# Reordering products, sums and MLP work at the seams of a fused attention and GELU-MLP kernel

## The chip, the cores and the metric

The kernel runs on one core of one Trainium2 chip. The metric is device time in microseconds (us) for one execution, as the median of several runs. The engines have these short names in the profile: PE is TensorE (matrix products; PEld its weight loads), DVE is VectorE, ACT is ScalarE, POOL is GpSimd, SP is SyncE, which here issues DMA transfers.

## The reference: what is computed

Threshold attention over 8 batches, 8 heads, 576 tokens and 64 columns a head, then a two-layer MLP with exact GELU on the 4608 resulting rows of 512. All of it is float32. Cut to what matters:

```python
scores = scale * q @ k.T                                  # per batch and head, 576 x 576
scores = where(scores >= max(scores) - tau, scores, -1e9)
attn   = exp(scores - max(scores)); attn /= (sum(attn) + 1e-9)
x      = (attn @ v) laid out as 4608 x 512
h      = x @ w_in                                         # 512 -> 2048, "layer one"
g      = 0.5 * h * (1 + erf(h / sqrt(2)))
out    = g @ w_out                                        # 2048 -> 512, "layer two"
```

## The kernel before

The kernel has two parts. In the first, attention runs pair of heads by pair of heads (32 pairs of 5 slots each: 160 slots). For each pair the exponentials are transposed through DMA into tiles pT, and `weigh_v` multiplies them with v into x^T in PSUM; ACT copies it to `xall`, and POOL divides it by the row sums. In between, a pacing function (`GOAL`, `fill`) feeds PE with plain MLP products for the blocks of 256 tokens that are complete: `hT` is layer one, `o_ps` layer two. It handles 8 of the 18 blocks.

The second part, `last_blocks`, does the other 10 blocks in two groups of five, with a seven-product multiplication (Strassen's scheme in Winograd's form): fewer products on PE, paid for with sums of operands. Layer one uses it on two levels (seven outer products, each a chain of seven products with 320 columns), layer two on one level. Each group has four steps j; a step is layer one (`layer_in`), then layer two (`layer_out`) for a quarter of the hidden columns. The pieces that the change touches:

```python
    def x_sums():

        room = list(tail["x_room"])
        x = xall[:, 0:len(AWAY), :, :].rearrange("p b (k h) (o t) -> p b k h o t", k=2, o=2)
        part = {f"b{k + 1}{o + 1}": x[:, :, k, :, o, :] for k in range(2) for o in range(2)}
        right = tail["right"] = {}

        def inner(eng, name, v, keep=False):
            b = {(h, i): v[:, :, h, i * RUN:(i + 1) * RUN] for h in range(2) for i in range(2)}
            t1, t2, t4 = (room.pop(0) for _ in range(3))
            t3 = room.pop(0) if keep else b[0, 1]
            right[name] = {"b11": b[0, 0], "b21": b[1, 0], "b22": b[1, 1], "t1": t1, "t2": t2, "t3": t3, "t4": t4}
            yield eng, lambda: sub(eng, t1, b[0, 1], b[0, 0])
            yield eng, lambda: sub(eng, t3, b[1, 1], b[0, 1])
            yield eng, lambda: sub(eng, t2, b[1, 1], t1)
            yield eng, lambda: sub(eng, t4, b[1, 0], t2)

        def outer(eng, out, a, b):
            for h in range(2):
                yield eng, lambda h=h: sub(eng, out[:, :, h, :], a[:, :, h, :], b[:, :, h, :])

        t1, t2, t4 = tail["t_x"]
        yield from outer(vec, t1, part["b12"], part["b11"])
        yield from inner(vec, "b11", part["b11"])
        yield from inner(vec, "t1", t1, True)
        yield from outer(vec, t2, part["b22"], t1)
        yield from inner(vec, "t2", t2, True)
        yield from outer(vec, part["b12"], part["b22"], part["b12"])
        yield from inner(vec, "t3", part["b12"])
        yield from inner(vec, "b22", part["b22"])
        yield from outer(vec, t4, part["b21"], t2)
        yield from inner(pool, "b21", part["b21"])
        yield from inner(pool, "t4", t4)
# ...
def taken(to, x, first):
        if first is None:
            nc.scalar.copy(to, x)
        else:
            add(vec, to, first, x)

waiting = []      # the two products of a chain that are issued inside the next one
beside = []       # sums that are issued one by one between products

    def step(which):

        if which is not None:
            which()
        if beside:
            beside.pop(0)[1]()
        while beside and beside[0][0] is pool:
            beside.pop(0)[1]()

    def chain(n, m, takes, done=None, runs=1):

        x, y = bank("sc", n), bank("mm", n)
        v = bank("mm", n) if "m2" in m else None

        def one_of(name, to, start):
            def run():
                product(to.rearrange("p (b t) -> p b t", b=runs) if runs > 1 else to, m[name], start)
                for t in takes[name]:
                    taken(t[0], to, t[1])
                if done:
                    done(name)
            return run

        before = waiting.pop(0) if waiting else (None, None)
        step(one_of("m1", x, True))
        step(before[0])
        step(one_of("m7", y, True))
        if v is not None:
            step(one_of("m2", v, True))
        step(before[1])
        step(one_of("m6", x, False))
        step(one_of("m4", y, False))
        waiting.append((one_of("m5", x, False), one_of("m3", x, False)))
# ... layer_in: seven outer chains; the last one is outer("s4", "b22", U, U, gelus_of(U))
    def g_sums():

        c, g = tail["c"], tail["g"]
        for t in range(2):
            g11, g21, g12, g22 = (c[:, i, :, t, :] for i in range(4))
            gs1, gs2 = g[:, 0, :, t, :], g[:, 1, :, t, :]
            yield vec, lambda gs1=gs1, a=g21, b=g22: add(vec, gs1, a, b)
            yield vec, lambda g21=g21, a=g11: sub(vec, g21, a, g21)
            yield vec, lambda gs2=gs2, a=gs1, b=g11: sub(vec, gs2, a, b)
            eng = (vec, pool)[t]
            yield eng, lambda eng=eng, g12=g12, b=gs2: sub(eng, g12, g12, b)

    def spread(items):
        for eng, run in items:
            yield eng, run
            if eng is vec:
                yield vec, lambda: None
# ... layer_out, with MT = 5 row tiles and HD = 256 columns:
        before = waiting.pop(0)
        for m in range(MT):
            v = bank("mm", HD)

            def run(m=m, v=v):
                product(v, rows(g12, m, w(1, 0)), True)
                taken(lo[m][:, 0:HD], v, None if first else lo[m][:, 0:HD])

            if m == 0:
                sums = list(g_sums())
                sums.pop(0)[1]()
            step(run)
            if m < 2:
                step(before[m])
            if m == 1:
                beside.extend(sums[:2])
                beside.extend(spread(sums[2:]))
        between(-1)
        for m in range(MT):
            l0, l1, h0, h1 = lo[m][:, 0:HD], lo[m][:, HD:2 * HD], hi[m][:, 0:HD], hi[m][:, HD:2 * HD]
            new = (lambda d: (d, None if first else d))
            takes = {"m1": [(l0, l0)], "m7": [new(h1)], "m6": [new(h0)], "m4": [(h0, h0)], "m5": [(h1, h1)], "m3": [new(l1)]}
            ms = {"m1": rows(g11, m, w(0, 0)), "m7": rows(g21, m, t[:, 2]), "m6": rows(gs2, m, t[:, 1]),
                  "m4": rows(g22, m, t[:, 3]), "m5": rows(gs1, m, t[:, 0]), "m3": rows(g12, m, w(1, 1))}

            def done(name, m=m):
                if final and name == "m5":
                    store(1, m)
                if final and name == "m3":
                    store(0, m)

            chain(HD, ms, takes, done)
            between(m)
# ... last_blocks:
        x_tiles()
        sums = list(x_sums())
        for _, run in sums[:10]:
            run()
        w_out_sums(vec, 0)
        for _, run in sums[10:]:
            run()
# ...
                if m == 0 and after[1] != j:
                    beside.append((pool, lambda j=after[1]: w_in_sums(pool, j)))
                if m == 0 and after[0] != n:
                    beside.extend(x_sums())

            layer_in(j, in_layer_in)
            layer_out(GROUPS[n], j, in_layer_out, at % NJ == 0, at % NJ == NJ - 1)
# ... the pacing of plain MLP work in the attention part (BATCH * B = 160 slots, WEIGH = 2, PLAIN = 8):
    GOAL = [(-1, 0.0), (START - 1, 0.0), (BATCH - 1, 0.42)]
    GOAL += [(BATCH * (m + 2) + DIVIDE, x) for m, x in enumerate([1.92, 2.89, 3.86, 4.82, 5.79, 6.75])]
    GOAL += [(BATCH * B + WEIGH, PLAIN - 0.28)]
```

How to read it. A *product* on PE writes a PSUM bank, and `taken` moves or adds the bank to SBUF: an ACT copy where the target is new, a DVE addition otherwise. A chain has two banks x and y that accumulate: m1, then m6, m5, m3 go into x, m7 and m4 into y, and m2, which layer two's chains lack, has a bank of its own. So each product must wait until the take before it has read the bank. m5 and m3 of a chain are not issued with it; they wait in `waiting` and are issued inside the next chain. At the seam from layer one to layer two, the next "chain" is the loop over five tiles m, whose products (g12 times a block of w_out) need nothing of the last chain. `g_sums` are eight sums of GELU results that layer two needs (four for each half t). `step` runs one product and then takes one sum from `beside`.

Of the kernel before, what the change touches and what calls it, by code (L numbers as in the profile page):

```python
# [18 lines left out]
def kernel(  # L19
# [31 lines left out]
    B, H, S, D = q.shape  # L51
# [16 lines left out]
    PLAIN = N_BLK - 10  # L68
# [61 lines left out]
    sums = [att.tile([P, Q], FP32, name=f"sums{i}") for i in range(2)]  # L130
# [532 lines left out]
    def sub(eng, out, a, b):  # L663
        eng.tensor_tensor(out, a, b, op=ALU.subtract)  # L664
# [46 lines left out]
    def w_out_sums(eng, j):  # L711
        t = tail["t"]
        b11, b12 = w_out_q[:, 0, :, j, 0:HD], w_out_q[:, 0, :, j, HD:2 * HD]
        b21, b22 = w_out_q[:, 1, :, j, 0:HD], w_out_q[:, 1, :, j, HD:2 * HD]
        sub(eng, t[:, 0], b12, b11)
        sub(eng, t[:, 1], b22, t[:, 0])
        sub(eng, t[:, 2], b22, b12)
        sub(eng, t[:, 3], b21, t[:, 1])
# [29 lines left out]
# [17 lines that stand above are left out]
        def outer(eng, out, a, b):  # L765
            for h in range(2):
                yield eng, lambda h=h: sub(eng, out[:, :, h, :], a[:, :, h, :], b[:, :, h, :])

        t1, t2, t4 = tail["t_x"]
        yield from outer(vec, t1, part["b12"], part["b11"])  # L770
# [11 lines that stand above are left out]
    def product(to, pairs, start):  # L782
        for k, (l, r) in enumerate(pairs):
            nc.tensor.matmul(to, lhsT=l, rhs=r, start=start and k == 0, stop=k == len(pairs) - 1,  # L784
                             skip_group_check=not start)

    def bank(tag, n):
        if tag == "sc":
            return ps.tile([P, 2, 512], FP32, tag="sc", name="bank", bufs=2)[:, 0, 0:n]
        return ps.tile([P, 512], FP32, tag="mm", name="bank")[:, 0:n]  # L790
# [8 lines that stand above are left out]
    waiting = []  # L799
    beside = []  # L800
# [9 lines that stand above are left out]
# [87 lines left out]
# [6 lines that stand above are left out]
    def layer_out(blocks, j, between, first, final):  # L903

        c, g, t, o = tail["c"], tail["g"], tail["t"], tail["o"]
        g11, g21, g12, g22 = (c[:, i].rearrange("p f t n -> p f (t n)") for i in range(4))
        gs1, gs2 = (g[:, i].rearrange("p f t n -> p f (t n)") for i in range(2))
        lo, hi = o[:MT], o[MT:]

        def rows(z, m, w):  # L910
            return [(z[:, f, m * P:(m + 1) * P], w[:, f]) for f in range(2)]

        def w(k, d):
            return w_out_q[:, k, :, j, d * HD:(d + 1) * HD]

        def store(half, m):
            for r in range(2):
                q, b = divmod(2 * m + r, len(AWAY))
                row = blocks[b] * TOK + (2 * half + q) * RUN
                nc.sync.dma_start(out[row:row + RUN, :], o[half * MT + m][r * RUN:(r + 1) * RUN, :])  # L920
# [10 lines that stand above are left out]
                sums = list(g_sums())  # L931
                sums.pop(0)[1]()
            step(run)
            if m < 2:
                step(before[m])
            if m == 1:
                beside.extend(sums[:2])
                beside.extend(spread(sums[2:]))
        between(-1)
        for m in range(MT):  # L940
            l0, l1, h0, h1 = lo[m][:, 0:HD], lo[m][:, HD:2 * HD], hi[m][:, 0:HD], hi[m][:, HD:2 * HD]
# [14 lines that stand above are left out]
    def last_blocks():  # L956

        assert set(x_free) == {XSLOTS - 2, XSLOTS - 1}
        GROUPS[0].sort(key=x_at.get)
        x_tiles()  # L960
        sums = list(x_sums())
        for _, run in sums[:10]:
            run()
        w_out_sums(vec, 0)
        for _, run in sums[10:]:
            run()
        steps = [(n, j if n % 2 == 0 else NJ - 1 - j) for n in range(len(GROUPS)) for j in range(NJ)]
        for at, (n, j) in enumerate(steps):
            before = steps[at - 1] if at else None
            after = steps[at + 1] if at + 1 < len(steps) else None  # L970

            def in_layer_in():
                if before and before[1] != j:
                    w_out_sums(pool, j)

            def in_layer_out(m):
                if after is None:
                    return
                if m == -1 and after[0] != n:
                    for k in range(2):  # L980
                        for b, x in enumerate(GROUPS[after[0]]):
                            nc.sync.dma_start(xall[:, b, 2 * k:2 * k + 2, :], away[x][:, 2 * k:2 * k + 2, :])
# [7 lines that stand above are left out]
        while waiting:  # L990
            for f in waiting.pop(0):
                f()
        assert not beside
# [25 lines left out]
    BATCH = HP * SLOTS  # L1019
    WIDE = 5 * 2 * Q  # L1020
    WEIGH = 2
# [2 lines left out]

    GOAL = [(-1, 0.0), (START - 1, 0.0), (BATCH - 1, 0.42)]
    GOAL += [(BATCH * (m + 2) + DIVIDE, x) for m, x in enumerate([1.92, 2.89, 3.86, 4.82, 5.79, 6.75])]
    GOAL += [(BATCH * B + WEIGH, PLAIN - 0.28)]

    def goal(n):
        for (lo, x), (hi, y) in zip(GOAL, GOAL[1:]):  # L1030
# [134 lines left out]
```

## Time and profile before

| what | value |
|---|---|
| median of 3 runs | 1365.79 us (1365.21 to 1366.95) |
| span of the profiled execution | 1365.8 us, 20074 instructions |
| busy: PE / DVE / POOL / ACT | 1338.9 / 1066.8 / 634.4 / 600.3 us |
| attention with plain MLP work | 0 to about 896 us |
| the two groups in seven-product form | about 896 to 1366 us |

The profile page gives first the busy time of each engine, then the span in 40 slices with the busy tenths of each engine and the clock that TensorE was granted, then DMA, then the chain of waits that ended last, then the costliest groups of instructions. For this case the timeline (each instruction, or run of equal ones, with its start and duration) is the view that matters. In it a float32 product on PE shows as two records. Records start one after another at a fixed pitch and their ends are modelled, so a run of n records has a length of (n-1) pitches and one duration.

### The profile page before, as it was taken

How to read it: one execution, taken by the hardware profiler on the slowest of the kernel's cores; microseconds unless marked ns; L12 is line 12 of the kernel's file. 1: busy time of each engine (PE TensorE's matmuls, PEld its weight loads, DVE VectorE, ACT ScalarE, POOL GpSimd, SP SyncE). 2: the span in 40 equal slices, each digit the busy share in tenths (PEclk: the TensorE clock that was granted, in tenths of full speed). 3: DMA queues.
4: the chain of work that ended last, by engine and by line, in shares of the span. 5: the costliest groups of instructions: out<-in, count | busy, mean ns of one | idle time of the engine just before them, and what ended most of it. 6: DMA issues, size and time to landing. Idle time of an engine off the chain costs nothing.

```text
span 1365.8 us, 20074 instructions
## 1 busy us (share of the span) xinstructions
PE 1338.9 (98%) x6398; PEld 904.1 (66%) x6398; DVE 1066.8 (78%) x2062; ACT 600.3 (44%) x1024; POOL 634.4 (46%) x1085
## 2 busy tenths in 40 slices
PE   8899999999999999999999999999999999999998
PEld 6677557466466566556557557468787777877777
DVE  7998777788888888878988888863857698385665
ACT  7766537438447448448538448222201113210120
POOL 5553344454555565555555541235264503635530
PEclk9999999999999999999999999999999999999999
DMA  9987376677777787787787785400000131000003
GB/s 293 327 307 216 78 165 142 140 169 181 160 183 168 164 205 163 166 213 156 164 216 158 167 188 115 104 9 1 0 1 0 39 91 26 1 1 0 1 0 78
DMA packets 212471, 169.18 MB, mean 124 GB/s; under 512 B 113872, under 2 KB 193600, under 8 KB 212368
## 3 DMA queue, kind: packets, MB, share of 16 engines
q1 hardware_dynamic: 188224, 112.53, 37.3%
q0 software_dynamic: 23712, 55.08, 13.4%
q8 instruction: 52, 0.85, 0.3%
q14 instruction: 51, 0.42, 0.1%
q10 hardware_dynamic: 432, 0.30, 0.1%
HBM read 72.73 MB, written 12.52 MB: 62 GB/s over the span
## 4 chain that ended last, share of the span: by engine, by line
PE 84%; DVE 8%; DMA 3%; SPq 2%; ACT 1%; issue 1%; POOL 0%; DVEq 0%; ACTq 0%; POOLq 0%
PE bank L784 30%; PE hT L597 16%; PE o_ps L612 15%; PE sc L403 12%; PE xT L521 10%; PE tr L345 1%; DVE o L667 1%; DMA turned_p<-in_moe_w_in_dram 1%; DVE nmx L415 1%; DVE p L434 1%; DVE c L667 1%; DMA x<-xall 1%; DVE c L664 1%; DVE power L217 1%; ACT p L418 1%
## 5 line engine op out<-in xcount | busy, mean ns | idle before, releaser
L418 ACT ACTIVATE p<-sc,nmx 128x576 f32<-128x576 f32 x288 | 201.5, 737 | 267.1 <-DVE nmx L415 266.7
L434 DVE SCALAR_TENSOR_TENSOR p<-sc,thr,p 128x576 f32<-128x576 f32 x288 | 225.2, 815 | 64.5 <-ACT p L418 61.4
L416 POOL TENSOR_SCALAR thr<-nmx,tau_eff 128x1 f32<-128x1 f32 x288 | 89.1, 309 | 375.6 <-DVE nmx L415 374.7
L415 DVE TENSOR_REDUCE nmx<-sc 128x1 f32<-128x576 f32 x288 | 205.2, 749 | 53.9 <-PE sc L403 52.8
L597 PE MATMUL hT<-xall,w_in 128*128 128x256 f32 x1024 | 241.9, 386 | 0.0
L612 PE MATMUL o_ps<-w_out,g 128*128 128x512 f32 x512 | 238.4, 606 | 0.0
L597 PEld LDWEIGHTS hT<-xall,w_in 128*128 128x128 f32 x1024 | 189.3, 190 | 51.0 <-issue 25.4
L667 DVE TENSOR_TENSOR c<-c,bank 128x320 f32<-128x320 f32 x304 | 147.3, 487 | 44.5 <-PE bank L784 30.8
L667 DVE TENSOR_TENSOR o<-o,bank 128x256 f32<-128x256 f32 x240 | 100.6, 419 | 95.0 <-PE bank L784 94.5
L612 PEld LDWEIGHTS o_ps<-w_out,g 128*128 128x128 f32 x512 | 93.8, 191 | 110.7 <-issue 108.3
L521 PE MATMUL xT<-pT,v 128*64 128x256 f32 (+1 forms) x1280 | 164.8, 410 | 2.2 <-DMA pT<-pd_tail 2.2
L403 PE MATMUL sc<-kT,qT 64*128 64x288 f32 x960 | 159.0, 430 | 3.0 <-DVE p L434 2.4
L482 DVE STREAM_TRANSPOSE turned_p<-p 128x1152 f32<-128x1152 f32 x112 | 154.4, 1378 | 3.9
L403 PEld LDWEIGHTS sc<-kT,qT 64*128 64x128 f32 x960 | 91.1, 186 | 76.3 <-issue 62.6
L521 PEld LDWEIGHTS xT<-pT,v 128*64 128x64 f32 x1280 | 89.4, 137 | 74.6 <-issue 13.3
L784 PE MATMUL bank<-w_out,c 128*128 128x256 f32 x480 | 119.8, 380 | 1.0 <-DVE o L667 0.7
L265 POOL DMA_DIRECT2D v<-in_v_dram x208 | 110.9, 536 | 4.0 <-issue 2.0
L784 PEld LDWEIGHTS bank<-w_out,c 128*128 128x128 f32 x480 | 90.3, 190 | 19.0 <-DVE o L667 2.4
L837 ACT ACTIVATE c<-c 128x320 f32<-128x320 f32 (+1 forms) x80 | 46.9, 623 | 112.1 <-DVE c L667 112.0
L667 POOL TENSOR_TENSOR c<-c,g 128x320 f32<-128x320 f32 (+1 forms) x40 | 50.5, 1271 | 79.1 <-DVE c L667 79.1
L784 PE MATMUL bank<-t_out,g 128*128 128x256 f32 x320 | 82.8, 381 | 1.6 <-DVE o L667 1.6
L795 ACT COPY c<-bank 128x320 f32<-128x320 f32 x32 | 13.6, 425 | 159.5 <-PE bank L784 159.4
(181 smaller groups left out, 1858.5 us busy)
## 6 DMA issues: line engine op xcount, KB each, us to landing
pT<-turned_p SPq DMA_DIRECT2D x448, 160.0 KB, 3.6
pT<-pd_tail SPq DMA_DIRECT2D x112, 80.0 KB, 3.1
q<-in_q_dram POOLq DMA_DIRECT2D x104, 72.0 KB, 3.2
k<-in_k_dram POOLq DMA_DIRECT2D x104, 72.0 KB, 3.3
inv<-turned SPq DMA_DIRECT2D x54, 128.0 KB, 4.0
v<-in_v_dram POOLq DMA_DIRECT2D x156, 40.0 KB, 3.2
out_dram<-o SPq DMA_DIRECT2D x40, 128.0 KB, 2.4
xall<-in_moe_w_out_dram POOLq DMA_DIRECT2D x9, 512.0 KB, 4.8
```

The costliest lines, as they stand in the source:

```text
L265: eng.dma_start(t[r:P:4, e, 0:n, :], rows[:, r * KR:r * KR + n, :])
L403: nc.tensor.matmul(sc[e][:, h, 0:HALF], lhsT=lhsT, rhs=s["kT"][rows, at:at + HALF], start=True, stop=True)
L415: nc.vector.tensor_reduce(nmx[:, e:e + 1], sc, axis=AXIS.XY, op=ALU.max, negate=True)
L416: nc.gpsimd.tensor_scalar(thr[:, e:e + 1], nmx[:, e:e + 1], -1.0, tau_eff, op0=ALU.mult, op1=ALU.subtract)
L418: nc.scalar.activation(w[:, e * S:(e + 1) * S].rearrange("p (h s) -> p h s", h=2), sc, AF.Exp, bias=nmx[:, e:e + 1], scale=1.0)
L434: nc.vector.scalar_tensor_tensor(row, sc[e][:, :, 0:HALF], thr[:, e:e + 1], row, op0=ALU.is_ge, op1=ALU.mult, accum_out=den[e])
L482: nc.vector.transpose(turned_p[:, :, i // 2, 0:NB, i % 2 * Q:(i % 2 + 1) * Q], w.rearrange("p (e b i) -> p e b i", e=2, i=Q))
L521: nc.tensor.matmul(to, lhsT=s["v"][:, e, c, :], rhs=rhs, start=(c == 0), stop=(c == KR - 1))
L597: nc.tensor.matmul(hT[:, j % 2, :], lhsT=w_in_sb[c][:, j * P:(j + 1) * P], rhs=x_blk[n][:, c, :], start=(c == 0), stop=(c == N_DM - 1))
L612: nc.tensor.matmul(o[:, 0:d_model], lhsT=g[j][:, m * P:(m + 1) * P], rhs=w_out_sb[j], start=(j == 0), stop=(j == N_DF - 1))
L667: eng.tensor_tensor(out, a, b, op=ALU.add)
L784: nc.tensor.matmul(to, lhsT=l, rhs=r, start=start and k == 0, stop=k == len(pairs) - 1, skip_group_check=not start)
```

## The change: what it does and what it is for

There are three parts.

1. **At the seam from layer one to layer two.** Of the last chain of layer one two products are left over, m5 and m3. Before, they stood behind the first and second tile of layer two; now they stand behind the first and third. The second and third sum of `g_sums` are issued by themselves behind tiles 1 and 2, and the other five go into `beside`, each vector one with an empty place after it. The aim is to give the take of m5 time before m3 needs its bank, and to keep sums from standing in front of takes.
2. **Sums of x for the second group.** In `x_sums` each sum of `outer` (the wide ones, 640 columns) is followed by an empty place, so that two wide sums are not issued in two steps in a row. The count of sums that run at once ahead of the first group goes from 10 to 12 for that reason alone: two of the 12 are empty places.
3. **Pacing.** The goal of MLP work is raised for the slots 159 to 161, so that more plain MLP work is done ahead of the x^T product of the last pair, which waits for DMA, and less behind it.

The instructions are the same in number and kind; only their order differs. On PE, the products between the last scores (`sc` from q_tail) and the x^T of the last pair are 21 `o_ps` instead of 9, and those behind it 10 instead of 21; one `hT` product more and one `o_ps` fewer stand ahead of those scores.

```diff
@@ -765,6 +765,7 @@
         def outer(eng, out, a, b):
             for h in range(2):
                 yield eng, lambda h=h: sub(eng, out[:, :, h, :], a[:, :, h, :], b[:, :, h, :])
+                yield eng, lambda: None
 
         t1, t2, t4 = tail["t_x"]
         yield from outer(vec, t1, part["b12"], part["b11"])
@@ -931,11 +932,11 @@
                 sums = list(g_sums())
                 sums.pop(0)[1]()
             step(run)
-            if m < 2:
-                step(before[m])
-            if m == 1:
-                beside.extend(sums[:2])
-                beside.extend(spread(sums[2:]))
+            if m % 2 == 0 and m < 4:
+                step(before[m // 2])
+            if m in (1, 2):
+                sums.pop(0)[1]()
+        beside.extend(spread(sums))
         between(-1)
         for m in range(MT):
             l0, l1, h0, h1 = lo[m][:, 0:HD], lo[m][:, HD:2 * HD], hi[m][:, 0:HD], hi[m][:, HD:2 * HD]
@@ -959,10 +960,10 @@
         GROUPS[0].sort(key=x_at.get)
         x_tiles()
         sums = list(x_sums())
-        for _, run in sums[:10]:
+        for _, run in sums[:12]:
             run()
         w_out_sums(vec, 0)
-        for _, run in sums[10:]:
+        for _, run in sums[12:]:
             run()
         steps = [(n, j if n % 2 == 0 else NJ - 1 - j) for n in range(len(GROUPS)) for j in range(NJ)]
         for at, (n, j) in enumerate(steps):
@@ -1024,7 +1025,7 @@
 
     GOAL = [(-1, 0.0), (START - 1, 0.0), (BATCH - 1, 0.42)]
     GOAL += [(BATCH * (m + 2) + DIVIDE, x) for m, x in enumerate([1.92, 2.89, 3.86, 4.82, 5.79, 6.75])]
-    GOAL += [(BATCH * B + WEIGH, PLAIN - 0.28)]
+    GOAL += [(BATCH * B - 1, PLAIN - 0.44), (BATCH * B + 1, PLAIN - 0.17), (BATCH * B + WEIGH, PLAIN - 0.17)]
 
     def goal(n):
         for (lo, x), (hi, y) in zip(GOAL, GOAL[1:]):
```

## The prediction, made before the result was known

> **What bounds the kernel now.** I read the page's first two parts, then the timeline of PE and of DVE at one seam of the second part, then the same around the last x^T, and the chain of waits to see whether the pattern repeats.
>
> ```profile
> PE 1338.9 (98%) x6398; PEld 904.1 (66%) x6398; DVE 1066.8 (78%) x2062; ACT 600.3 (44%) x1024; POOL 634.4 (46%) x1085
> PE   8899999999999999999999999999999999999998
> ```
>
> PE is the bound throughout: 1365.8 - 1338.9 leaves 27 us of idle time, part of it at the two ends. No PE work is removed by the change, so all it can win is holes on PE, and they are small. To size them I go by the pitch of starts. A run of 16 records with 256 columns (second fence) takes 3.62 us, the last of them 0.38, so (3.62 - 0.38) / 15 = 0.216 us each; records of 320 columns in the same way (4 in 1.24 us, the last 0.43) 0.27, and a 512-column `o_ps` record 0.43. A product of layer two is 4 records, 0.86 us; one of layer one 2 records, 0.54 us.
>
> PE at the second seam of its kind, group one, step j = 2:
>
> ```profile
> 1036.87 1.03 PE L784 MATMUL bank<-w_out,c 128*128 128x256 f32 x4
> 1037.73 0.70 PE L784 MATMUL bank<-x,s_in 128*128 128x320 f32 x2
> 1038.27 1.03 PE L784 MATMUL bank<-w_out,c 128*128 128x256 f32 x4
> 1039.75 0.81 PE L784 MATMUL bank<-xall,s_in 128*128 128x320 f32 x2 [0.46 <-DVE c L667]
> 1040.39 3.62 PE L784 MATMUL bank<-w_out,c 128*128 128x256 f32 x16
> 1043.85 1.03 PE L784 MATMUL bank<-t_out,c 128*128 128x256 f32 x4
> 1045.14 1.13 PE L784 MATMUL bank<-t_out,g 128*128 128x256 f32 x4 [0.26 <-DVE o L667]
> 1046.20 1.13 PE L784 MATMUL bank<-t_out,c 128*128 128x256 f32 x4
> ```
>
> These are tile 0, m5, tile 1, m3, then tiles 2 to 4 and m1 of the first layer-two chain, m7, m6, m4. Tile 1 should be over at 1038.27 + 0.86 = 1039.13, but m3 starts at 1039.75 and its run is 0.1 longer: 0.72 lost. m6 should start at 1043.85 + 0.86 = 1044.71, starts at 1045.14, and each of the two rows from there is stretched by 0.1, with 0.1 more between them (1045.14 + 0.96 = 1046.10 against 1046.20): another 0.72. DVE in the same place:
>
> ```profile
> 1038.14 0.83 DVE L667 TENSOR_TENSOR g<-c 128x640 f32<-128x640 f32 x1 [0.54 <-ACT c L837]
> 1038.89 0.41 DVE L667 TENSOR_TENSOR o<-o,bank 128x256 f32<-128x256 f32 x1
> 1039.22 0.48 DVE L667 TENSOR_TENSOR c<-c,bank 128x320 f32<-128x320 f32 x1
> ...
> 1043.60 0.41 DVE L667 TENSOR_TENSOR o<-o,bank 128x256 f32<-128x256 f32 x1
> 1043.93 0.82 DVE L664 TENSOR_TENSOR c<-c,g 128x640 f32<-128x640 f32 x1
> 1044.67 0.41 DVE L667 TENSOR_TENSOR o<-o,bank 128x256 f32<-128x256 f32 x1
> ```
>
> The take of m5 (1039.22) stands behind the first sum, which waits for a GELU; m3 goes into the same bank and starts when that take ends at 1039.7. The take of m1 (1044.67) stands behind the sum at 1043.93, and m6 starts when it ends. So 1.44 us are lost here. The chain of waits has the same rows at 981, 1039, 1097, 1214, 1272 and 1330 us; at the two seams with new output tiles (924 and 1157, where ACT takes the tiles) only the first wait stands, 0.40 us each. All eight: 6 x 1.44 + 2 x 0.40 = 9.4 us.
>
> The last x^T, with an undisturbed one (849.39) to compare:
>
> ```profile
> 849.39 5.07 PE L521 MATMUL xT<-pT,v 128*64 128x320 f32 x40
> ...
> 868.96 3.34 PE L521 MATMUL xT<-pT,v 128*64 128x320 f32 x22
> 874.47 3.36 PE L521 MATMUL xT<-pT,v 128*64 128x256 f32 x18 [2.18 <-DMA pT<-pd_tail]
> ```
> ```profile
> 875.00:876.00 1.00, 1.00 (x12) 0.74 (x10) 1.00 (x2) 0.00 (x0) 0.83 (x1) 0.82 0.00 0
> 876.00:877.00 1.00, 1.00 (x7) 0.67 (x4) 0.96 (x3) 0.00 (x0) 0.00 (x0) 0.50 0.00 0
> 877.00:878.00 1.00, 1.00 (x4) 0.24 (x3) 0.97 (x4) 0.13 (x1) 0.00 (x0) 0.50 0.00 0
> 878.00:880.00 2.00, 2.00 (x4) 0.98 (x5) 1.97 (x3) 0.24 (x1) 1.68 (x2) 0.73 0.00 0
> ```
>
> PE waits 2.2 us for the last transposed tile. Then the granted clock (the number before the last two) is halved: 0.18 + 0.50 + 0.50 + 2 x 0.27 = 1.7 us of full clock lost. Together 3.9 us.
>
> The fourth place is the end of group one (1107 to 1125), where wide sums of x stand between takes: four late products of layer two, by the same pitch count 0.46, 0.34, 0.38 and 0.32, and 0.16 shortly after: 1.7 us.
>
> [...] The half clock here lasts 1.7 / 0.5 = 3.4 us[...]. [...] the take of tile 0, complete at about 1037.9 (1036.87 + 1.03), starts at 1038.89 only, behind a sum that waits. [...] a wide sum takes 0.82 us alone and 1.48 at 1107.49, beside a POOL sum. [...]
>
> **Part 1, the seams.** PE from 1036.87 with the new order, if nothing waits: tile 0, m5 at 1037.73, tile 1 at 1038.27, tile 2 at 1039.13, m3 at 1039.99, tile 3 at 1040.53, tile 4 at 1041.39, m1 at 1042.25, m7 at 1043.11, m6 at 1043.97, m4 at 1044.83. A bank is ready for its take about 0.75 us after the start of a 320-column product (0.70 + 0.04) and 1.07 after a layer-two product. DVE occupies per instruction, by the distances of starts above, 0.33 us for a tile's take, 0.40 for a layer-one take, 0.74 for a sum. In the new order, from 1038.89: tile 0, m5 (1039.22), tile 1 (1039.62), second sum (1039.96), tile 2 (1040.69), m3 (1041.03), third sum (1041.43), tile 3 (1042.17), tile 4 (1042.50), m1 (1043.32, when ready), fourth sum (1043.65), m7 (1044.39). m3 needs the take of m5: over at 1039.70, before 1039.99. m6 needs the take of m1: over at 1043.73, before 1043.97. m4 needs the take of m7: over at 1044.80, just before 1044.83. The third sum, which m6 reads, is over at 1042.2. One chain on, the leftover m3 needs a take that my walk ends 0.1 us too late. I keep 0.1 us a seam for that and the narrow m4: 6 x 1.34 = 8.0, and 0.8 for the other two seams, **8.8 us**.
>
> **Part 2, spaced wide sums.** Every empty place gives DVE one step (0.86 us) with only a 0.33 take. The tight spot is m3 of each chain: m5 is two steps ahead of it, so 1.72 - 1.07 - 0.41 = 0.24 us of slack for the take of m5. In the new order no wide sum falls between m7 and the take of m5 in layer two, so I expect nearly no loss there. But 8 more places push 14 instead of 5 vector sums and places past the end of layer two into the next layer one, whose steps are 0.54 us. There two wide sums, the second beside POOL (1.44 us in the trace now), come just ahead of a take that m3 of the second chain needs, about 0.6 us too late. Estimate: 1.7 now, 0.9 after, **0.8 us**.
>
> **Part 3, MLP work ahead of the last x^T.** Its start moves by 11 `o_ps` x 0.86 + one `hT` (2 x 0.215) = 9.9 us, to 878.9. Its second half then starts at about 881.6, and its data were there at 874.4: no wait, no half clock. x^T lasts 5.0 as at 849.39 (to 854.39, the next row), the 10 `o_ps` behind it 8.6: layer one starts at 868.96 + 9.9 + 5.0 + 8.6 = 892.5 instead of 896.5: **4.0 us**, as the 3.9 above.
>
> **Sum.** 8.8 + 0.8 + 4.0 = 13.6 us, so 1352.2; I say 1352.5.
>
> **The rivals.** (a) *The wait moves.* The change takes nothing off DVE, and the walk passes m4 by 0.03 us. If takes start only a little later, the loss of the first wait goes and that of the second stays, 6 x 0.72 = 4.3 us less gain: 1356.8. For it: DVE is without a pause from 1038.1 to 1042.8 in my walk. Against it: the old order has four sums ahead of m6, the new one three. (b) *DVE becomes late at the start of the first group.* x^T comes 6 us later in time, and DVE's second wide sum waits for it: it can go on at about 885.6 instead of 882.8, and the sums end at 894.7 instead of 891.9, while layer one starts at 892.5. Its first takes are mostly ACT copies and the first DVE take is due at 894.9, so I expect nothing; if I am wrong, 1 to 2 us, 1354. (c) *The half clock stays* although the wait goes, since earlier stretches have it too (clock 0.98 and 0.97 in the first 200 us): 1.7 us, 1354. (d) *The overflow of sums into the second group costs more* than spacing wins, because POOL's sums start some 5 us later: 1 to 2 us. In each rival the bound stays PE, and none reaches the time of before.
>
> **Range and chances.** The holes named add up to 9.4 + 1.7 + 3.9 = 15.0 us, so 1350.8 is the floor; with the spread of the measurement (1.7 us over three runs) I take 1350.5. Rivals (a) alone, or two of the small ones, give 1356 to 1357: 1356.8 as the upper end. 2% is 27 us, more than all of PE's idle time, so within 2% has 0.98, and faster or slower by more 0.01 each.
>
> **What would show it.** In the timeline after: m3 and m6 at the seams without idle ahead of them; x^T of the last pair in one unbroken run of about 5 us with a clock of 1.00 around it; the first row of layer one at about 892.5; at the group change no late products in layer two, one or two small ones in the first chains behind it. I am wrong if m4 or m6 still wait for DVE at each seam, or if ACT or DVE holds the first chains of layer one.

## The result, and the profile after

The median is 1354.66 us (1353.78 to 1355.1) against 1365.53 us of the kernel before (four executions, the three of the table above among them); the ratio is 0.9918, with a 95% interval of 0.99 to 0.9935. The prediction said 1352.5 us, between 1350.5 and 1356.8. The changed kernel was timed twice more: 0.9905 (0.9889 to 0.9922) and 0.9921 (0.9902 to 0.994). So the gain is 10.9 us by the first medians and 11 to 13 by the ratios, where my sum was 13.6; between the two profiles it is 12.6 (1365.8 to 1353.2).

First the page's busy line and, from the chain of waits, the one row that covers nearly all of the second part, both of the kernel after:

```profile
PE 1334.1 (99%) x6398; PEld 905.6 (67%) x6398; DVE 1063.0 (79%) x2062; ACT 600.7 (44%) x1024; POOL 633.7 (47%) x1085
```
```profile
893.06 454.11 PE bank L785 x1900
```

In the chain of before, each seam broke the PE rows with takes, sums and a GELU. Now PE is released by nothing but itself from 893 to 1347 us. The same seam as in the prediction (group one, j = 2), timeline of PE after; columns: start, duration, engine, line, operation, tiles, shape, records:

```profile
1031.74 1.03 PE L785 MATMUL bank<-w_out,c 128*128 128x256 f32 x4
1032.61 0.70 PE L785 MATMUL bank<-x,s_in 128*128 128x320 f32 x2
1033.14 1.89 PE L785 MATMUL bank<-w_out,c 128*128 128x256 f32 x8
1034.87 0.70 PE L785 MATMUL bank<-xall,s_in 128*128 128x320 f32 x2
1035.41 2.75 PE L785 MATMUL bank<-w_out,c 128*128 128x256 f32 x12
1038.00 1.03 PE L785 MATMUL bank<-t_out,c 128*128 128x256 f32 x4
1038.86 1.03 PE L785 MATMUL bank<-t_out,g 128*128 128x256 f32 x4
1039.74 1.13 PE L785 MATMUL bank<-t_out,c 128*128 128x256 f32 x4
```

Tiles 1 and 2 run as one row of 8, m3 follows at once (1033.14 + 8 x 0.216 = 1034.87), and m6 (1038.86) comes one product after m7. Only m4 (1039.74) is 0.02 late and 0.1 longer. The last x^T, after:

```profile
879.21 5.07 PE L521 MATMUL xT<-pT,v 128*64 128x320 f32 x40
884.21 8.85 PE L612 MATMUL o_ps<-w_out,g 128*128 128x512 f32 x20
892.89 0.70 PE L785 MATMUL bank<-xall,w_in 128*128 128x320 f32 x2
```

It is one unbroken run of 5.0 us to the next start, and layer one starts at 892.89. The clock (the number before the last two) is 1.00 in this stretch, where it fell to 0.50 before:

```profile
880.00:885.00 5.00, 5.00 (x38) 2.79 (x35) 1.05 (x2) 0.86 (x3) 1.23 (x3) 1.00 0.00 0
```

Two lengths in the trace separate the parts from the spread of executions. One goes from the start of the x^T of the last pair but one to the first product of layer one, and is 47.1 us before (849.39 to 896.52) and 43.1 after (849.76 to 892.89). The other goes from the start of the first to the start of the last product record of the second part: 464.5 before, 455.5 after. The start of that x^T itself lay anywhere from 846.9 to 852.5 us in the profiles, in kernels that are the same up to there: of the differences between profiles of equal work this is the largest, and it blurs the times. The first product of layer one, before:

```profile
896.52 0.70 PE L784 MATMUL bank<-xall,w_in 128*128 128x320 f32 x2
```

### The profile page after: what moved, and what is told of

The parts are those of the page before. It is cut to its first block, busy times and chain, and to the rows that moved or that the text cites. A ratio compares the mean times of both kernels' runs of the same rounds, so it can differ in the third digit from the quotient of the medians.

```text
span 1353.2 us, 20076 instructions
## 1 busy us (share of the span) xinstructions
PE 1334.1 (99%) x6398; PEld 905.6 (67%) x6398; DVE 1063.0 (79%) x2062; ACT 600.7 (44%) x1024; POOL 633.7 (47%) x1085
## 4 chain that ended last, share of the span: by engine, by line
PE 93%; DMA 3%; DVE 2%; SPq 1%; ACT 1%; issue 0%; POOL 0%; ACTq 0%; DVEq 0%; POOLq 0%
PE bank L785 34%; PE o_ps L612 17%; PE hT L597 17%; PE sc L403 13%; PE xT L521 11%; PE tr L345 2%; DMA v<-in_v_dram 1%; DMA x<-xall 1%; DMA xall<-in_moe_w_in_dram 1%; DMA k<-in_k_dram 1%; DVE p L434 0%; DVE nmx L415 0%; ACT p L418 0%; DVE power L217 0%; SPq L284 0%
## 5 line engine op out<-in xcount | busy, mean ns | idle before, releaser
L785 PE MATMUL bank<-t_out,c 128*128 128x256 f32 x320 | 82.7, 381 | 0.0
```

## The experiments

All ratios are to the kernel before on the same chip. The last two columns are the two lengths just named, from the profile of each run; those of timed executions are not known.

| kernel | ratio (95% interval) | x^T to layer one, us | second part, us |
|---|---|---|---|
| before_again | 1.0002 (0.999 to 1.0013) | 45.0 | 464.5 |
| pacing_only | 0.9973 (0.9963 to 0.9983) | 43.1 | 464.5 |
| seam_only | 0.994 (0.9922 to 0.9957) | 45.6 | 456.1 |
| spacing_only | 0.9987 (0.9977 to 0.9998) | 45.2 | 463.3 |
| products_only | 0.9967 (0.9956 to 0.9978) | 44.9 | 459.3 |
| sums_only | 0.9968 (0.996 to 0.9976) | 44.9 | 461.3 |
| wait_long | 1.0029 (1.0018 to 1.004) | 47.8 | 464.6 |
| after_again / after_third | 0.9905 / 0.9921 | 43.1 | 455.6 |
| tuned / tuned2 / tuned3 | 0.9909 (0.9894 to 0.9924) / 0.9934 (0.9915 to 0.9952) / 0.9902 (0.9884 to 0.992) | 43.1 | 455.0 / 454.9 / 454.2 |

**The kernel before once more** (no edit).

> The kernel before, unchanged, profiled and timed once more. The saving was 12.6 us between the two profiles (1365.8 to 1353.2) but 10.9 us between the medians. Theory A (the number of half-clock windows of 3.4 us differs between executions, 1.7 us each, wherever they fall): ratio 1.000 within noise, its executions spread over 1 to 3 us, and the longer ones have the lower mean clock (0.00125 per window). Theory B (the half clock behind the 2.2 us wait for the last x^T is itself there in some executions only): this profile shows a clock of 1.00 between 875 and 880 us and a span near 1364. If instead the half clock stands there again, A alone holds.

Its profile lasts 1364.2 us, 1.6 less than the first. Timeline of PE, then two stretches (start and end, length, busy time and records of each engine, clock, DMA share, GB/s):

```profile
869.53 3.34 PE L521 MATMUL xT<-pT,v 128*64 128x320 f32 x22
874.58 2.34 PE L521 MATMUL xT<-pT,v 128*64 128x256 f32 x18 [1.72 <-issue]
```
```profile
872.00:876.00 4.00, 2.28 (x20) 1.47 (x18) 3.93 (x9) 0.49 (x2) 1.02 (x3) 1.00 0.39 70
876.00:880.00 4.00, 4.00 (x16) 1.82 (x13) 3.93 (x6) 0.37 (x1) 2.53 (x3) 1.00 0.00 0
```

The wait is there (1.7 us), the half clock is not: the 18 records take 2.34 us instead of 3.36. So theory B holds for this execution: the half clock behind the wait belongs to some executions only. Theory A agrees with the times beside it: executions of before with mean clock 0.993 took 1368.9 us on average, those with 0.996 1365.8 (8 and 9 of the 45 timed beside `wait_long`).

**Each part alone.**

```diff
# pacing_only: the GOAL line of the change, nothing else
# seam_only: the lines of layer_out of the change, nothing else
# spacing_only: the empty place in outer(), and 12 for 10
```

> Part 3 alone: more plain MLP work ahead of the last x^T; seams and x sums as before. If the wait and the half clock behind it are both always there before, it gains 4.0 us in the trace and in time (1361.5). If the half clock is there in some executions only, the time falls by 2.2 to 3 us (1362.5 to 1363.3). If DVE coming late to the first chains cost something (rival b), by 1 to 2 us less, and the trace shows PE waiting for DVE or ACT between 892 and 905 us. Second part of the trace as before: about 12 us of holes.

> Part 1 alone: products and sums at the seams; pacing and x sums as before. Holes at the eight seams fall from 9.4 us to about 1.6 (0.2 at each of eight, as in the trace of the changed kernel), so a gain of about 7.9 us, to 1357.7. If the gains of the parts overlap (the rival: DVE catches up by itself once one of the parts is there), it gains 9 or more and the three parts add up to more than the 10.9 of all.

> Part 2 alone: empty places behind the wide x sums. In the trace the late products at the group change fall from 1.7 us to 0.5, a gain of 1.2 us (1364.3). My prediction had 0.8, with 0.6 lost in the second chain of layer one; if that is so here, the trace shows a product there 0.6 us late. The rival (overflow of sums costs more than it wins) has 1366 to 1367.

Pacing: 43.1 us in place of 44.9 to 45.6 where a profile of the old pacing had no half clock, or of 47.1 where it had: 1.8 to 2.5 us, or 4.0. In time it wins 3.7 us (2.3 to 5.1), and its mean clock is 0.9954 against 0.9948 of before, half a half-clock stretch fewer in an execution (one stretch of 3.41 us at a clock of 0.50, as at 875.65 us in the first profile of before, is 0.00125 of 1366 us). Both would fit a half clock that stood behind the wait in a part of the timed executions; neither is sharp enough to show it. No wait for DVE or ACT shows at the start of layer one. Seams: 464.5 - 456.1 = 8.4 us in the trace, 8.2 in time (5.9 to 10.7). Spacing: 464.5 - 463.3 = 1.2 us in the trace, 1.8 in time (0.3 to 3.1). The parts' gains in the second part, 8.4 + 1.2, are 0.6 more than the 9.0 of both together; the overlap is at the change of group, where the seam edit alone already brings the holes from 1.7 to 1.1 us. In time the three parts alone add up to 3.7 + 8.2 + 1.8 = 13.7 us, more than the 11 to 13 of all, but within the intervals. The largest hole that the spacing closes is in layer two of the kernel before: a product that should start at 1109.54 + 0.86 = 1110.40 starts at 1110.76.

```profile
1109.54 1.03 PE L784 MATMUL bank<-t_out,c 128*128 128x256 f32 x4
1110.76 1.13 PE L784 MATMUL bank<-w_out,c 128*128 128x256 f32 x4 [0.20 <-DVE o L667]
```

**The seam edit taken apart.**

```diff
# products_only, against before
-            if m < 2:
-                step(before[m])
+            if m % 2 == 0 and m < 4:
+                step(before[m // 2])
# sums_only, against before
-            if m == 1:
-                beside.extend(sums[:2])
-                beside.extend(spread(sums[2:]))
+            if m in (1, 2):
+                sums.pop(0)[1]()
+        beside.extend(spread(sums))
```

> Of part 1 only the move of the second leftover product (m3) from the second to the third tile; the sums stand as before. Theory (the two waits at a seam have separate causes: m3 waits because only one tile lies between it and m5; m6 waits because sums stand ahead of the take of m1): the first hole (0.72 us at six seams, 0.40 at two) goes, 5.1 us; of the second, which now meets a PE that is 0.6 us further on, 0.3 to 0.7 us stays at each of six seams. Gain 4.5 to 7 us. Rival (DVE is the limit at the seam, so a hole that is closed opens again later): the second hole grows to 1.3 us or more and the gain is below 2 us.

> Of part 1 only the order of the sums; the two leftover products stand behind the first and second tile as before. Theory: the first hole stays (0.72 us at six seams, 0.40 at two), the second goes, a gain of 6 x 0.7 = 4.3 us. Rival as for the products alone: gain below 2 us.

Timeline of PE with the products alone, from m7 on:

```profile
1042.55 1.03 PE L784 MATMUL bank<-t_out,c 128*128 128x256 f32 x4
1043.70 1.13 PE L784 MATMUL bank<-t_out,g 128*128 128x256 f32 x4
1044.76 1.13 PE L784 MATMUL bank<-t_out,c 128*128 128x256 f32 x4
```

and with the sums alone, tile 1, m3 and m6:

```profile
1033.23 1.03 PE L784 MATMUL bank<-w_out,c 128*128 128x256 f32 x4
1034.71 0.81 PE L784 MATMUL bank<-xall,s_in 128*128 128x320 f32 x2 [0.46 <-DVE c L667]
...
1039.67 1.03 PE L784 MATMUL bank<-t_out,g 128*128 128x256 f32 x4
```

With the products alone m3 is on time and m6 still late (1043.70 against 1042.55 + 0.86 = 1043.41, and two stretched rows), about 0.6 us a seam. With the sums alone m3 is late by the same 0.62 as before and m6 on time (1038.81 + 0.86). So at a seam the two holes have separate causes, and closing the first doesn't open the second further (0.6 us against 0.72): there the rival is out. For the sums I had expected 4.3 us; 0.2 us a seam stayed, as with both edits.

The second parts are 5.2 and 3.2 us shorter. That the sum, 8.4, is what both edits win is partly chance. By the pitch of starts, the holes of the eight seams fall from 9.5 us to 3.5, 6.6 and, with both, 1.5, so here the two edits overlap by some 0.9 us. In return, with the products alone the holes at the change of group grow from 1.7 to 2.4 us, where the other two kernels have 1.1. A leftover m3, due at 1104.64 + 0.86 = 1105.50, comes 0.98 late, so that there something of the rival does show:

```profile
1104.64 1.03 PE L784 MATMUL bank<-t_out,c 128*128 128x256 f32 x4
1106.48 1.13 PE L784 MATMUL bank<-w_out,c 128*128 128x256 f32 x4 [0.81 <-DVE o L667]
```

**A longer wait.**

```diff
-    GOAL += [(BATCH * B + WEIGH, PLAIN - 0.28)]
+    GOAL += [(BATCH * B - 1, PLAIN - 0.43), (BATCH * B + WEIGH, PLAIN - 0.35)]
```

> The kernel before with 3 o_ps products fewer between the last scores and the last x^T, and 3 more behind it, so that PE waits some 2.6 us longer for the same transfer (about 4.5 us). From the x^T of the last pair but one to layer one the executions of the kernel before took 45.0 to 45.6 us without the half clock and 47.1 with it. Theory [...]: [...] the half clock is there for certain: 45.1 + 2.6 + 1.7 = 49.4 us. If the half clock is by chance whatever the wait: 47.7 in an execution without it.

```profile
868.28 3.37 PE L521 MATMUL xT<-pT,v 128*64 128x320 f32 x20 [0.64 <-DMA pT<-turned_p]
873.14 0.62 PE L521 MATMUL xT<-pT,v 128*64 128x256 f32 x2 [1.49 <-DMA pT<-pd_tail]
875.37 2.34 PE L521 MATMUL xT<-pT,v 128*64 128x256 f32 x18 [1.62 <-issue]
```

The stretch is 47.8 us, 2.8 longer than in before_again: the wait in full, and no half clock. My "for certain" was wrong: the wait is broken by products whose data had come, into pieces of 0.64, 1.49 and 1.62 us, each shorter than the 2.18 us of the first profile of before; whether that is why no half clock followed is not shown. In time the kernel is 4.0 us slower (2.5 to 5.5), and the mean clock of its 20 timed executions is 0.9935 against 0.9946 of before; at 0.00125 a half-clock stretch, on average about one more fell somewhere in them. Where is not visible for executions that were not profiled.

**The changed kernel again, and three versions that go on from it.**

```diff
# tuned and tuned2, tuned3: before the five sums beside (tuned2, tuned3: not at the change of group)
+        beside.extend([(vec, lambda: None)] * 2)
# last chain: tuned   m1, (m5), m6, (m3), m5, m7, m3, m4
#             tuned2  m1, (m5), m7, m6, m4, m5, (m3), m3, last stores shared by SP and ACT queue
#             tuned3  as tuned2, but at the very end alone, not also at the end of group one
# (m5), (m3): the products left over from the chain before
```

> The changed kernel, unchanged, timed again on the same chip as the next one. From the parts in the traces, the last seams and x sums give 9.0 us, the pacing 2.0 us, or 3.7 where the half clock behind the wait is there: 11.0 to 12.7 us against the kernel before, a ratio near 0.991. If the 10.9 us of the first medians had been low by chance and my sum of 13.6 right, 0.990.

> The changed kernel with two further moves. The very last chain is issued as m1, m6, m5, m7, m3, m4 instead of m1, m7, m6, m4, m5, m3, so that a product lies between any two that share a bank: the hole of 0.78 us ahead of the last product goes. And two empty places stand ahead of the five sums that are issued beside, so that the fourth sum comes after the take of m7 and not ahead of it: the hole of 0.12 us at m4 goes at six seams, 0.7 us, and the one of 0.1 us at the leftover m3 stays or goes. In the trace the second part lasts 454.0 us from its first to its last product instead of 455.5. In time 1.5 us less, which lies at the edge of what five rounds resolve. Rival (the sums, one chain later, stand ahead of other takes): the holes of 0.1 us appear elsewhere and only the 0.78 at the end are won.

> The first tuned version won 0.52 us of the second part and lost 0.41 of it between the last product and the end; its sums came too late at the change of group (0.64 and 0.33 us there). Here the two empty places are left out at the change of group, and the last chain is issued as m1, m7, m6, m4, m5, the leftover m3 of the chain before, m3, with the stores of the last pieces shared between the SP and the ACT queue. If the reading of both losses is right: second part 454.0 us (455.5 in the changed kernel), last product to end 4.7 us as there, so 1.5 us less in the trace. If the end needs the last two stores in any case (rival), 5.1 us stay there and 1.1 us less remain.

> The changed kernel again, on the same chip as the second tuned version, as its comparison: second part 455.5 us, last product to end 4.7 us, ratio to the kernel before near 0.991.

> In both tuned versions the new issue order of the last chain also stood at the end of group one, where its two leftover products had been inside the next layer one; the holes there grew from 0.42 us to 1.07 and 1.00. Here it stands at the very end alone. Theory: the holes at the change of group fall back to 0.42 us, the second part lasts 454.2 us (455.5 in the changed kernel, 454.9 in the second tuned one), last product to end stays 5.1 us, so 0.9 us less than the changed kernel in the trace, too little to show in the medians. Rival (the spread at the change of group has another cause): 454.9 us as before.

What they are aimed at, in the timeline of PE after, is the last hole of size: m5, then m3 in the same bank with nothing between:

```profile
1346.13 1.03 PE L785 MATMUL bank<-t_out,g 128*128 128x256 f32 x4
1347.67 1.13 PE L785 MATMUL bank<-w_out,c 128*128 128x256 f32 x4 [0.51 <-DVE o L667]
```

All three close it, and the one at m4. `tuned` and `tuned2` lost part of that at the change of group (holes of 1.4 and 1.0 us against 0.4). The expectation of `tuned2` blamed the empty places; they account for 0.33 us of it, which `tuned2` no longer has. `tuned3` undoes two more things at the end of group one, the new order of the last chain and the stores on the ACT queue, and there the holes are 0.4 us and the second part is 454.2 us, as expected. Which of the two cost how much is not separated: `tuned` had the new order without such stores, but in `tuned2` 0.46 us of its 1.0 is a wait for an ACT copy that starts only behind them:

```profile
1119.32 2.49 ACTq L928 DMA_DIRECT2D out_dram<-o  x4
1121.91 0.75 ACT L796 COPY c<-bank 128x320 f32<-128x320 f32 x2 [28.12 <-DMA out_dram<-o]
```
```profile
1122.38 0.81 PE L785 MATMUL bank<-x,s_plain 128*128 128x320 f32 x2 [0.30 <-ACT c L796]
```

From the last product to the end it is 5.2 us in place of 4.7, with the stores on one queue or on two; why is left open. What remains of `tuned3` is 0.9 us in the trace. In time `tuned3` has the lowest ratio, 0.9902 (0.9884 to 0.992), but it can't be told from the changed kernel.

## Why the prediction was right, point by point

The time lies in the range, and the mechanism held at the seams, at the change of group and for the wait ahead of the last x^T; the sum was 1 to 3 us too large, in the traces by one term above all, the half clock.

- **Bound.** Right: PE stays the bound, and all of the gain is holes closed on it.
- **Seams: 8.8 us predicted.** The walk put m3 at 3.12 us, m6 at 7.10 and m4 at 7.96 us after tile 0; the trace has 3.13, 7.12 and 8.00. The holes at the eight seams went from 9.5 to 1.5 us, a gain of 8.0. Mis-sized is the rest I kept, 0.1 us at six seams: it is 0.2 there, since the narrow m4 (0.12) and the leftover m3 (0.10) both show, and 0.1 at the other two.
- **Spaced sums: 0.8 us predicted.** The holes at the change of group went from 1.7 to 0.4, a gain of 1.3. The 0.6 us in the second chain of layer one was the wrong term: the product is there, 0.12 late and 0.1 longer (timeline after, below). The two errors partly cancel, and the second part as a whole won 9.0 us where I had 9.6.

```profile
1128.38 0.70 PE L785 MATMUL bank<-t_x,s_out 128*128 128x320 f32 x2
1129.04 0.81 PE L785 MATMUL bank<-t_x,s_in 128*128 128x320 f32 x2
```

- **Pacing: 4.0 us predicted.** Between the two first profiles it is 47.1 - 43.1 = 4.0, but that is luck: the term of 1.7 us for the half clock was taken from one execution as if every one had it. Of seven profiles with the old amount of work ahead of x^T, or less (before twice, seam_only, spacing_only, products_only, sums_only, wait_long), only the first shows it (47.1 us to layer one; 44.9 to 45.6 in the others, and in wait_long the 18 records in 2.34 us). Without it the step is worth 1.8 to 2.5 us in the traces. This is the term most wrong in size: by the traces without the half clock, all of the change is worth 9.0 + 1.8 to 2.5, some 11 us, near the 10.9 of the first medians. The times don't confirm this split: `pacing_only` alone won 3.7 us (2.3 to 5.1), close to the 4.0, so how often the half clock stood there in timed executions is open.
- **Rivals.** (a) fell: both waits go. (b) fell: layer one starts with an unbroken row of products though DVE's sums end at 895.5 us instead of 891.9. (c) was half the truth: the half clock near x^T is gone in after, where the wait is gone (clock 1.00), but it was not always there before; others stand at 46 to 160 us in both kernels, three in the first profile of before and four in that of after (the one more at 61 us). (d) fell: the overflow costs some 0.4 us in layer one (0.2 at 1125.05 and 0.2 at 1129.04), less than the spacing wins.

## What to carry to other kernels

When a chain reuses one accumulator, write down the time from a product's start to the end of its take (here 1.07 + 0.41 = 1.48 us for 256 columns, against 0.86 us a product) and put at least that much independent work between two products of the bank; and put no sum in front of a take that a product is about to need. Work that is free to move belongs ahead of a wait for a transfer, not behind it (here worth 1.8 to 4.0 us). Before a clock dip goes into a sum, look whether a second profile has it.

## What the runs showed of the hardware that I had not expected

Ahead of the last product, half-clock stretches in the first profile of before start at 46.21, 128.13, 158.85 and 875.65 us, in that of after at 47.70, 61.35, 129.62 and 160.34; each lasts 3.41 us at a clock of 0.50. The one at 875.65 comes behind a wait of 2.18 us for the last x^T, 1.18 us after PE has gone on (874.47).

Behind shorter waits for the last x^T none followed: 1.86 us in `spacing_only` and 1.72 in `before_again`, where the 18 records took 2.34 us each time. In `wait_long` the three waits add up to 3.75 us, the longest of them 1.62, and none followed either (clock 1.00 from 866 to 882 us). So the sum of the waits does not decide alone whether a half clock follows, and one profile that shows it there is too few to name a limit for a single wait; what decides it is open.
